# Keys of 30 heads in one load each, with the last 112 tiles copied aside by ScalarE

## The chip, the cores and the metric

The kernel runs on one core of a Trainium2 chip. The metric is the device time of one execution in microseconds (us). The median of three runs before the change is 1277.63 us (1277.61 to 1277.86).

## The reference

One token goes through a layer with attention over cached keys and values and then a small dense block. There are 32 heads of 128 elements and 32768 cached positions; the keys and the values of one head are 8 MB each in bf16, 537 MB in all.

```python
x = A_x                                              # 1 x 1 x 512
q = (layernorm(x) @ wq).reshape(32 heads, 128)
scores = einsum("bhqd,bhkd->bhqk", q, k_cache) * 128 ** -0.5
o = einsum("bhqk,bhkd->bhqd", softmax(scores), v_cache)
h = x + o.reshape(1, 1, 4096) @ wo                   # wo: 4096 x 512
t = layernorm(h) @ w1 + b1                           # w1: 512 x 1376
out = h + (t * tanh(softplus(t))) @ w2               # w2: 1376 x 512
```

## The kernel before

All large operands live in `ring`, six slots of 32 KB per partition. Slots 0 and 1 take the two halves of a head's keys, slots 2 and 3 its values, slot 4 first `wq` and at the end `w1` and `w2`, and slot 5 `wo`. Partition p holds 256 consecutive positions of the cache (`"(p r) d -> p (r d)"`), so a head's keys are 256 tiles of 128 x 128, 128 tiles in each half. A half is one load with 32 KB in a row per partition; the values of a head are one load with 64 KB in a row.

All large loads are issued by SyncE, in the order of the list `order`: `wq`, then for every head both halves of the keys and the values, then `wo` in four pieces, `w1` in two and `w2` in four. SyncE's queue (SPq in the profile) is strictly in order, so a load that waits holds back all behind it. `freed_by` says what a load waits for: a half of the keys for the last transposes of the same half of the head before, the values for the last matmul on the values of the head before (`pv`), `w1` and `w2` for the last use of `wq` (`qm32`). `wo` waits for nothing, since its slot is empty until then.

For each head (`one`, a loop over 32 heads in the programs of TensorE, VectorE and ScalarE) TensorE goes through 32 groups of eight tiles (`k_group`). It transposes the eight tiles (L456) into one of four PSUM buffers, VectorE copies them to `ering` (L459), and three groups later TensorE multiplies them with the query (L433, `scores`). Then come the maximum (L482 to L499), the exponential on ScalarE (L502), the sum (L507) and 256 matmuls of values with probabilities (L470, `pv`). In this loop ScalarE has nothing but the exponential. After the last head TensorE brings the 32 outputs into place (L535, L539) and runs `wo` (L549), the second layernorm, `w1` (L564) and `w2` (L583). POOL writes to a scratch row `skip` only in order to count a semaphore up where a load has one part instead of two.

Of the kernel before, what the change touches and what calls it, by code (L numbers as in the profile page):

```python
# [7 lines left out]
F32 = mybir.dt.float32  # L8
# [5 lines left out]
PE, ACT, DVE, POOL, SP = "pe", "act", "dve", "pool", "sp"  # L14
# [156 lines left out]
def build_kernel(nc, A_x, A_k_cache, A_v_cache, A_wq, A_wo, B_w1, B_b1, B_w2, out):  # L171
    D = A_x.shape[-1]
    Dh = 128
    HD = A_wq.shape[1]
    H = HD // Dh
# [9 lines left out]
    TPS = 128  # L185
    SLOT = TPS * Dh
    HALVES = Sk // (128 * TPS)
    SCOLS = HALVES * TPS
    GT = 8
    GPS = TPS // GT  # L190
    NE = 4
    NT = 4
    KEEP = 3
    FJ = F // 128
    FLAST = F - FJ * 128
    W1 = KC * F
# [7 lines left out]
    def sb(shape, dt, name):  # L204
        cm = nc.sbuf_tensor(name, shape, dt)
        t = cm.__enter__()
        allocs.append(cm)
        return t.ap()
# [7 lines left out]
    ring = sb([128, NS, SLOT], BF16, "ring")  # L216
# [4 lines left out]
    nb = sb([128, 1], F32, "nbias")  # L221
    esum = sb([128, 1], F32, "esum")
    pmax = sb([128, 1], F32, "pmax")
    rtotc = sb([128, 1], F32, "rtotc")
    gmax = sb([1, 1], F32, "gmax")
    skip = sb([1, H], F32, "skip")
    identi = sb([128, 128], I32, "identi")
    ident = sb([128, 128], F32, "ident")
    identb = sb([128, 128], BF16, "identb")
# [34 lines left out]
    OX_PS = T_f[2][:, 0:32]  # L264

    sem = nc.alloc_semaphore
    kinds = [PE, ACT, DVE, POOL, SP, "exp", "pmax", "gmax", "qc", "A", "B", "C", "pv", "nb", "rcp", "qm"]
    kinds += [f"{k}{i}" for i in range(2 * GPS) for k in ("ev", "tr", "qk")]
    sems = {k: sem(f"s_{k}") for k in kinds}
    ready = [sem(f"ready{i}") for i in range(NS)]  # L270
# [11 lines left out]

    order = [("wq", 0)]
    for h in range(H):
        order += [("k", h, half) for half in range(HALVES)]
        order.append(("v", h))
    order += [("wo", n) for n in range(len(s_wo))] + [("w1", n) for n in range(len(s_w1))] + [("w2", n) for n in range(len(s_w2))]

# [5 lines left out]
    def ready_wait(what):  # L294
        return (ready[slot_of(what)], 16 * (what[1] + 1 if what[0] in "kv" else 1))

    def free_name(what):
        return "free" + "_".join(map(str, what))

    def freed_by(what):  # L300
        if what[0] in ("w1", "w2"):
            return [f"qm{H}"]
        if what[0] in "kv" and what[1] > 0:
            return [free_name((what[0], what[1] - 1) + what[2:])]
        return []

    def flat_of(what):
        if what[0] == "v":
            return ring[:, HALVES:2 * HALVES, :].rearrange("p s x -> p (s x)")
        return ring[:, slot_of(what), :]  # L310

    def tiles_of(what):
        return flat_of(what).rearrange("p (r d) -> p r d", d=Dh)

    wq_v = ring[:, slot_of(("wq",)), :].rearrange("p (k n) -> p k n", k=KC)
    wo_f = ring[:, slot_of(("wo",)), :]
# [7 lines left out]
    def program(S):  # L324
        t_ = nc.tensor
        a = nc.scalar
        v = nc.vector
        g = nc.gpsimd
# [3 lines left out]
        def start(dst, src, s):  # L332
            S.dma(SP, lambda: sp.dma_start(dst, src).then_inc(s, 16))  # L333

        for what in order:
            slot = slot_of(what)
            S.wait(SP, freed_by(what))
            flat = flat_of(what)
            if what[0] == "wq":
                start(flat, A_wq.rearrange("(p k) n -> p (k n)", k=KC), ready[slot])  # L340
            elif what[0] == "wo":
                j0, j1 = WO_J[what[1]:what[1] + 2]
                start(wo_f[:, j0 * D:j1 * D], A_wo.rearrange("(p j) n -> p (j n)", j=32)[:, j0 * D:j1 * D], s_wo[what[1]])
            elif what[0] == "w1":
                k0, k1 = W1_K[what[1]:what[1] + 2]
                start(w1_v[:, k0:k1, :], B_w1[k0 * 128:k1 * 128, :].rearrange("(k p) n -> p k n", p=128), s_w1[what[1]])
            elif what[0] == "w2":
                j0, j1 = W2_J[what[1]:what[1] + 2]
                if j1 <= FJ:
                    start(w2_v[:, j0:j1, :], B_w2[j0 * 128:j1 * 128, :].rearrange("(j p) n -> p j n", p=128), s_w2[what[1]])  # L350
                else:
                    start(w2_v[0:FLAST, FJ, :], B_w2[FJ * 128:F, :], s_w2[what[1]])
            else:
                cache = A_k_cache if what[0] == "k" else A_v_cache
                rows = cache[0, what[1], :, :].rearrange("(p r) d -> p (r d)", r=SCOLS)
                at = what[2] * SLOT if what[0] == "k" else 0
                if what == ("v", H - 1):
                    start(flat[:, 0:SLOT], rows[:, 0:SLOT], ready[slot])
                    start(flat[:, SLOT:], rows[:, SLOT:], s_half)
                else:  # L360
                    start(flat, rows[:, at:at + flat.shape[-1]], ready[slot])
        S.dma(SP, lambda: sp.dma_start(out[0, 0, :].rearrange("(c m) -> c m", c=KC), outr[0:128:32, :]).then_inc(s_out, 16),
              waits=["fin"])
# [8 lines left out]
        if S.emit and S.only == POOL:  # L372
            for n in range(H - 1):
                g.memset(skip[:, n:n + 1], 0.0).then_inc(s_half, 16)
        S.step(POOL, lambda: g.iota(seli[:, :, :], [[-1, WB], [1, 128]], base=0, channel_multiplier=-WB), name="seli")
        S.step(POOL, lambda: g.memset(b1r[:, :], 0.0), name="b1z")
        S.dma(POOL, lambda: g.dma_start(b1r[0:FJ, :], B_b1[0:FJ * 128].rearrange("(j p) -> j p", j=FJ)).then_inc(s_b1, 16),
              waits=["b1z"])
        S.dma(POOL, lambda: g.dma_start(b1r[FJ:FJ + 1, 0:FLAST], B_b1[FJ * 128:F].rearrange("(o p) -> o p", o=1)).then_inc(s_b1, 16))
        S.step(DVE, lambda: v.memset(oT[:, :], 0.0), name="oTz")  # L380
        S.step(DVE, lambda: v.memset(onesm[:, :], 1.0), name="consts0")
        S.step(DVE, lambda: v.memset(epsc[:, :], EPS), name="epsc")
# [4 lines left out]
               waits=["identb", (s_x, 32)])  # L387
# [24 lines left out]
        for kc in range(KC):  # L412
            S.step(PE, lambda kc=kc: t_.matmul(Q_REG, wq_v[:, kc, 0:Dh], xnT[:, 0, kc:kc + 1], start=(kc == 0), stop=(kc == KC - 1)),
                   name=[f"qkb{kc - NE}"] + (["qm0"] if kc == KC - 1 else []), kind=f"qk{(kc - NE) % (2 * GPS)}",
                   waits=(["xn0", ready_wait(("wq", 0))] if kc == 0 else ()))
# [25 lines left out]
        def k_group(h, half, gi):  # L441
            what = ("k", h, half)
            bg = count[0]
            count[0] += 1
            kt = tiles_of(what)
            tb = T_b[bg % NT]
            for r in range(GT):
                waits = []
                if r == 0:
                    if gi == 0:  # L450
                        waits.append(ready_wait(what))
                    waits.append("identb")
                names = []
                if r == GT - 1:
                    names = [f"trb{bg}"] + ([free_name(what)] if gi == GPS - 1 else [])
                S.step(PE, lambda r=r: t_.matmul(tb[:, r * 128:(r + 1) * 128], kt[:, gi * GT + r, :], identb[:, :],  # L456
                                                 is_transpose=True, start=True, stop=True),
                       name=(names or None), waits=waits, kind=(f"tr{bg % (2 * GPS)}" if names else None))
            S.step(DVE, lambda: v.tensor_copy(ering[:, bg % NE, :, :].rearrange("p r d -> p (r d)"), tb[:, :]),  # L459
                   name=f"ev{bg}", waits=[f"trb{bg}", f"qkb{bg - NE}"],  # L460
                   kind=f"ev{bg % (2 * GPS)}")
            pend.append((h, half * TPS + gi * GT, bg))
            flush(KEEP)

# [46 lines left out]

        def one(n):
            h = n - 1
            for half in range(HALVES):
                for gi in range(GPS):
                    k_group(h, half, gi)
            flush(0)
            soft_max(h)
            soft_a(h)
            soft_b(h)  # L520
            soft_exp(h)
            pv(h, 0, 64)
            soft_c(h)
            pv(h, 64, SCOLS)
            oev(h)
# [5 lines left out]
        if S.emit and S.only == PE:  # L531
            S.hint = t_.mark_branch_hint_location("LikelyTaken")
        S.step(PE, lambda: t_.matmul(hid_ps, b1r[:, :], identb[0:FJ + 1, 0:FJ + 1], start=True, stop=False, skip_group_check=True),
               waits=[(s_b1, 32), f"exp{H - 1}"])
        S.step(PE, lambda: t_.matmul(OR_PS, oT[:, :], identb[:, :], is_transpose=True, start=True, stop=True),  # L535
               name="oRt", waits=[f"oev{H - 1}", "oTz"])
        S.step(DVE, lambda: v.tensor_copy(oR[:, :], OR_PS), name="oR", waits=["oRt"])
        for b in range(WB):
            S.step(PE, lambda b=b: t_.matmul(OX_PS, sel[:, b, :], oR[:, 32 * b:32 * b + 32], start=(b == 0), stop=(b == WB - 1)),  # L539
                   name=("oXs" if b == WB - 1 else None), waits=(["oR", "sel"] if b == 0 else ()))  # L540
        S.step(DVE, lambda: v.tensor_copy(oX[:, :], OX_PS), name="oX", waits=["oXs"])
        S.step(DVE, lambda: v.memset(hpad[:, :], 0.0), name="hpadz")
        for j in range(32):
            for c in range(KC):
                waits = ["oX"] if j == 0 and c == 0 else []
                if c == 0 and j in WO_J:
# [4 lines left out]
                    start=(j == 0 and c == 0), stop=last, skip_group_check=True),  # L551
                    name=("y" if last else None), waits=waits)
# [6 lines left out]
               waits=["hpad", f"exp{H - 1}"])  # L559
        for kc in range(KC):  # L560
            for j in range(FJ + 1):
# [4 lines left out]
                    start=False, stop=last, skip_group_check=True),  # L566
                    name=("hid" if last else None), waits=((["xn1"] if kc == 0 else []) + ([(s_w1[W1_K.index(kc)], 16)] if kc in W1_K else []) if j == 0 else ()))
# [8 lines left out]
        for j in range(FJ + 1):  # L576
# [4 lines left out]
            for c in range(KC):  # L581
# [51 lines left out]
```

## Time and profile before

| what | value |
|---|---|
| median of 3 runs | 1277.63 us |
| span of the profiled execution (its own time is given as this span alone) | 1275.6 us |
| bytes moved, mean rate over the span | 548.24 MB, 430 GB/s |
| TensorE busy with matmuls | 1020.0 us (80%) |
| VectorE busy | 716.0 us (56%) |
| ScalarE busy | 20.6 us (2%) |
| mean granted TensorE clock | 0.769 |

A row of the timeline has the start, the duration, the engine, the line, what is written and read and how many instructions are merged; in brackets stands the idle time before it and what ended that. "issue" is time in which an engine waited for nothing that the profile shows. A row of the chain of waits has the start, the duration and the work. In a row of groups the number behind the bar is the total busy time, then the mean of one instruction in ns. A row on a DMA queue has packets, MB and the time that the packets took, as a share of 16 engines over the stretch asked for; it exceeds 100% a little where packets overlap or reach over the stretch's end. A row of stretches gives the busy time of TensorE's matmuls, its weight loads, VectorE, ScalarE and POOL, then the granted clock, the DMA share and GB/s.

### The profile page before, as it was taken

To read this page: it belongs to the slowest core of one execution; us is meant where nothing else is said; L and a number is where in the kernel's file an instruction comes from. 1 tells how busy PE (TensorE), PEld (TensorE's weight loads), DVE (VectorE), ACT (ScalarE), POOL (GpSimd) and SP (SyncE) were. 2 spreads that over 40 slices of the span, in tenths; PEclk is the share of its full clock that TensorE was granted. 3 is DMA by queue.
4 is the path that set the end of the run, shared out by engine and by line. 5 is a ranking of instruction groups with operands and counts; after the bars stand their busy time and mean duration, and the time that the engine had idled before them with its cause. 6 is when DMAs were issued, how large, how long until landed. Compare 5 with 4: busy or idle time off the path is not lost.

```text
span 1275.6 us, 53362 instructions
## 1 busy us (share of the span) xinstructions
PE 1020.0 (80%) x25129; PEld 996.3 (78%) x25129; DVE 716.0 (56%) x1246; ACT 20.6 (2%) x70; POOL 3.3 (0%) x40
## 2 busy tenths in 40 slices
PE   3788877879777888777887778797778887788977
PEld 3688877879777878777887778797778887777876
DVE  3466544566545665445665446664456654456643
ACT  0000000000000000000000000000000000000000
POOL 1000000000000000000000000000000000000000
PEclk9788777787767887768886778877678877688866
DMA  9999999999999999999999999999999999999998
GB/s 417 416 429 439 434 434 428 432 432 439 432 436 424 436 432 439 432 428 428 438 442 430 427 430 431 437 444 427 430 428 432 440 439 427 424 434 433 438 427 350
DMA packets 16906, 548.24 MB, mean 430 GB/s; under 512 B 1952, under 2 KB 3328, under 8 KB 4096
## 3 DMA queue, kind: packets, MB, share of 16 engines
q1 hardware_dynamic: 16680, 548.09, 99.7%
q8 instruction: 8, 0.13, 0.0%
q10 hardware_dynamic: 152, 0.00, 0.0%
q0 software_dynamic: 64, 0.00, 0.0%
q14 instruction: 2, 0.02, 0.0%
HBM read 548.08 MB, written 0.00 MB: 430 GB/s over the span
## 4 chain that ended last, share of the span: by engine, by line
DMA 66%; PE 32%; SPq 1%; issue 1%; DVE 0%; ACT 0%; ACTq 0%
DMA ring<-in_A_k_cache_dram 65%; PE tps L456 25%; PE sps L433 6%; SPq L333 1%; DMA ring<-in_B_w_dram 1%; PE ops L470 1%; DVE ering L459 0%; PE hlp L492 0%; PE hlp L497 0%; PE tps L583 0%; DVE pmax L482 0%; PE hlp L507 0%; PE yps L485 0%; DVE ering L589 0%; DVE gmax L494 0%
## 5 line engine op out<-in xcount | busy, mean ns | idle before, releaser
L459 DVE COPY ering<-tps 128x1024 bf16<-128x1024 bf16 x1024 | 669.3, 691 | 129.3 <-PE tps L456 128.5
L456 PE MATMUL tps<-identb,ring 128*128 128x128 bf16 x8192 | 667.7, 232 | 76.4 <-DMA ring<-in_A_k_cache_dram 76.4
L456 PEld LDWEIGHTS tps<-identb,ring 128*128 128x128 bf16 x8192 | 522.0, 104 | 78.9 <-DMA ring<-in_A_k_cache_dram 78.9
L433 PE MATMUL sps<-qcur,ering 128*128 128x1 bf16 x8192 | 343.7, 164 | 11.0 <-DVE ering L459 6.7
L470 PEld LDWEIGHTS ops<-pbuf,ring 128*128 128x128 bf16 x8192 | 229.7, 105 | 134.4 <-issue 132.5
L470 PE MATMUL ops<-pbuf,ring 128*128 128x1 bf16 x8192 | 227.6, 165 | 132.4 <-DMA ring<-in_A_v_cache_dram 127.2
L433 PEld LDWEIGHTS sps<-qcur,ering 128*128 128x128 bf16 x8192 | 308.9, 97 | 14.0 <-DVE ering L459 9.4
L509 DVE RECIPROCAL rtotc<-hlp 128x1 f32<-128x1 f32 x32 | 5.4, 168 | 196.6 <-PE hlp L507 196.6
L477 DVE TENSOR_TENSOR oT<-ops,rtotc 128x1 f32 x32 | 5.1, 161 | 165.7 <-PE ops L470 165.7
L502 ACT ACTIVATE pbuf<-sps,nbias 128x256 bf16<-128x256 f32 x32 | 15.1, 473 | 1223.1 <-DVE nbias L499 1223.1
L497 PEld LDWEIGHTS hlp<-gmax,onesmat 1*128 1x128 f32 x64 | 12.0, 233 | 21.6 <-DVE gmax L494 21.6
L497 PE MATMUL hlp<-gmax,onesmat 1*128 1x1 f32 x64 | 14.8, 297 | 11.9 <-DVE gmax L494 11.9
L482 DVE TENSOR_REDUCE pmax<-sps 128x1 f32<-128x256 f32 x32 | 13.6, 424 | 14.3 <-PE sps L433 14.3
L507 PE MATMUL hlp<-esum,onesmat 128*128 128x1 f32 x64 | 18.1, 352 | 0.0
L485 PE MATMUL yps<-xnT,ring 128*128 128x1 bf16 x128 | 16.3, 172 | 0.0
L492 PE MATMUL hlp<-ident,pmax 128*1 128x128 f32 x64 | 12.4, 275 | 4.7 <-DVE pmax L482 3.4
L507 PEld LDWEIGHTS hlp<-esum,onesmat 128*128 128x128 f32 x64 | 16.1, 312 | 0.0
L494 DVE TENSOR_REDUCE gmax<-hlp 1x1 f32<-1x128 f32 x32 | 8.9, 279 | 11.9 <-PE hlp L492 11.9
L499 DVE TENSOR_SCALAR nbias<-hlp 128x1 f32<-128x1 f32 x32 | 5.0, 158 | 17.7 <-PE hlp L497 17.7
L485 PEld LDWEIGHTS yps<-xnT,ring 128*128 x128 | 12.3, 96 | 2.0
L492 PEld LDWEIGHTS hlp<-ident,pmax 128*1 128x1 f32 x64 | 2.7, 80 | 7.4 <-DVE pmax L482 7.4
L386 PE MATMUL hlp<-identb,xr 4*128 4x4 bf16 x1 | 0.2, 159 | 9.3 <-DMA xr<-in_A_x_dram 9.3
(61 smaller groups left out, 41.2 us busy)
## 6 DMA issues: line engine op xcount, KB each, us to landing
ring<-in_A_k_cache_dram SPq DMA_DIRECT2D x64, 4096.0 KB, 26.7
ring<-in_A_v_cache_dram SPq DMA_DIRECT2D x2, 4096.0 KB, 26.2
ring<-in_A_wq_dram SPq DMA_DIRECT2D x1, 4096.0 KB, 12.3
ring<-in_A_wo_dram SPq DMA_DIRECT2D x1, 1792.0 KB, 34.7
ring<-in_B_w_dram SPq DMA_DIRECT2D x2, 688.0 KB, 17.5
ring<-in_A_wo_dram SPq DMA_DIRECT2D x1, 1280.0 KB, 37.4
ring<-in_B_w_dram SPq DMA_DIRECT2D x2, 512.0 KB, 19.6
ring<-in_A_wo_dram SPq DMA_DIRECT2D x1, 768.0 KB, 38.8
```

Source lines behind the costliest of these rows:

```text
L333: S.dma(SP, lambda: sp.dma_start(dst, src).then_inc(s, 16))
L433: S.step(PE, lambda r=r: t_.matmul(S_ps[:, col0 + r:col0 + r + 1], ering[:, bg % NE, r, :], qcur[:, :], start=True, stop=True), name=(name ...
L456: S.step(PE, lambda r=r: t_.matmul(tb[:, r * 128:(r + 1) * 128], kt[:, gi * GT + r, :], identb[:, :], is_transpose=True, start=True, stop= ...
L459: S.step(DVE, lambda: v.tensor_copy(ering[:, bg % NE, :, :].rearrange("p r d -> p (r d)"), tb[:, :]), name=f"ev{bg}", waits=[f"trb{bg}", f ...
L470: S.step(PE, lambda r=r, last=last: t_.matmul(o_ps[:, 0:1], vt[:, r, :], pbuf[:, r:r + 1], start=(r == 0), stop=last), name=([free_name((" ...
L482: S.step(DVE, lambda: v.tensor_reduce(pmax[:, :], S_ps[:, 0:SCOLS], AXX, ALU.max), name=f"pmax{h}", waits=[f"qkh{h}"], kind="pmax")
L485: S.step(PE, lambda kc=kc: t_.matmul(Q_REG, wq_v[:, kc, bass.ds((S.index(h + 1) % H) * Dh, Dh)], xnT[:, 0, kc:kc + 1], start=(kc == 0), st ...
L492: S.step(PE, lambda: t_.matmul(A_REG, pmax[:, :], ident[:, :], start=True, stop=True), name=f"A{h}", waits=[f"pmax{h}", "ident"], kind="A")
L494: S.step(DVE, lambda: v.tensor_reduce(gmax[:, :], A_REG, AXX, ALU.max), name=f"gmax{h}", waits=[f"A{h}"], kind="gmax")
L497: S.step(PE, lambda: t_.matmul(B_REG, onesm[0:1, :], gmax[:, :], start=True, stop=True), name=f"B{h}", waits=[f"gmax{h}", "consts0"], kind ...
L502: S.step(ACT, lambda: a.activation(pbuf[:, :], S_ps[:, 0:SCOLS], ACTF.Exp, bias=nb[:, :], scale=SC, accum_out=esum[:, :]), name=f"exp{h}", ...
L507: S.step(PE, lambda: t_.matmul(C_REG, onesm[:, :], esum[:, :], start=True, stop=True), name=f"C{h}", waits=[f"exp{h}"], kind="C")
```

## The change

The keys of heads 1 to 30 come in one load over slots 0 and 1, with 64 KB in a row per partition. The first and the last head (0 and 31) keep two halves. For every head, also for these two, ScalarE copies the last 112 of the 256 tiles to slot 5, as soon as all keys of the head are there and TensorE is through with the copy of the head before. TensorE transposes groups 0 to 17 from the slots of the load and groups 18 to 31 from the copy. The next load of keys waits for the transposes of group 17 (`kfree`) and for the copy (`kc`). The loads of `wo`, whose slot is now in use, wait for the last transposes of the last head (`kend31`). POOL counts the second half's semaphore up for the 30 heads that have no second load.

```diff
+    CT = 112
+    CG = (2 * TPS - CT) // GT
...
-        order += [("k", h, half) for half in range(HALVES)]
+        order += [("k", h, half) for half in range(HALVES if h in (0, H - 1) else 1)]
...
-        if what[0] in "kv" and what[1] > 0:
-            return [free_name((what[0], what[1] - 1) + what[2:])]
+        if what[0] == "wo":
+            return [f"kend{H - 1}"]
+        if what[0] == "k" and what[1] > 0:
+            return [f"kfree{what[1] - 1}", f"kc{what[1] - 1}"]
+        if what[0] == "v" and what[1] > 0:
+            return [free_name((what[0], what[1] - 1))]
...
+    khome = ring[:, 0:HALVES, :].rearrange("p s x -> p (s x)")
+    kcopy = ring[:, 2 * HALVES + 1, 0:CT * Dh]
...
+                if what[0] == "k" and 0 < what[1] < H - 1:
+                    start(khome, rows, ready[slot])
...
+        S.wait(POOL, [(ready[1], 16)])
+        if S.emit and S.only == POOL:
+            for n in range(1, H - 1):
+                g.memset(skip[:, H + n:H + n + 1], 0.0).then_inc(ready[1], 16)
...
-            kt = tiles_of(what)
+            g0 = half * GPS + gi
+            kt = kc_tiles if g0 >= CG else k_tiles
+            t0 = (g0 - (CG if g0 >= CG else 0)) * GT
...
+                    if g0 == CG:
+                        waits.append(f"kc{h}")
...
+            S.step(ACT, lambda: a.copy(kcopy, khome[:, CG * GT * Dh:]), name=f"kc{h}", kind="kc",
+                   waits=[(ready[0], 16 * (h + 1)), (ready[1], 16 * (h + 1))] + [f"kend{h - 1}"])
```

On ScalarE, in the loop over heads, the program before has the exponential alone:

```order
L407 ACTIVATE lns<-lns 128x1 [waits s_act]
L93 UNCONDITIONAL_BRANCH
L502 ACTIVATE pbuf,esum<-sps,nbias 128x256 [waits s_nb]
L93 REGISTER_ALU
L93 COMPARE_AND_BRANCH
```

The changed program has the copy ahead of it (`s_tr31` counts the last transposes of a head, `ready0` and `ready1` the two halves' loads):

```order
L425 ACTIVATE lns<-lns 128x1 [waits s_act]
L93 UNCONDITIONAL_BRANCH
L93 ISA
L536 COPY ring<-ring 128x14336 [waits s_tr31,ready1,ready0]
L524 ACTIVATE pbuf,esum<-sps,nbias 128x256 [waits s_nb]
L93 REGISTER_ALU
L93 COMPARE_AND_BRANCH
```

The copy stands ahead of the exponential of the same head and waits for loads and for TensorE, not for VectorE.

On SyncE's queue the last loads before the change are these (`s_tr15` counts the last transposes of a first half, `s_pv` the end of a head's values, `s_qm` the last use of `wq`):

```order
L333 DMA ring<-in_A_k_cache_dram 128x16384 [waits s_tr15]
L333 DMA ring<-in_A_k_cache_dram 128x16384 [waits s_tr31]
L333 DMA ring<-in_A_v_cache_dram 128x16384 [waits s_pv]
L333 DMA ring<-in_A_v_cache_dram 128x16384
L333 DMA ring<-in_A_wo_dram 128x7168
L333 DMA ring<-in_A_wo_dram 128x5120
L333 DMA ring<-in_A_wo_dram 128x3072
L333 DMA ring<-in_A_wo_dram 128x1024
L333 DMA ring<-in_B_w_dram 128x2x1376 [waits s_qm]
```

In the changed program the same stretch, with the last whole load of keys and its values ahead, reads:

```order
L344 DMA ring<-in_A_k_cache_dram 128x32768 [waits s_kc,s_tr17]
L344 DMA ring<-in_A_v_cache_dram 128x32768 [waits s_pv]
L344 DMA ring<-in_A_k_cache_dram 128x16384 [waits s_kc,s_tr17]
L344 DMA ring<-in_A_k_cache_dram 128x16384
L344 DMA ring<-in_A_v_cache_dram 128x16384 [waits s_pv]
L344 DMA ring<-in_A_v_cache_dram 128x16384
L344 DMA ring<-in_A_wo_dram 128x7168 [waits s_tr31]
L344 DMA ring<-in_A_wo_dram 128x5120
L344 DMA ring<-in_A_wo_dram 128x3072
L344 DMA ring<-in_A_wo_dram 128x1024
L344 DMA ring<-in_B_w_dram 128x2x1376 [waits s_qm]
```

The two halves of the last head's keys are issued together, behind the copy of the head before, and the first piece of `wo` has a wait where it had none.

More of the change, by code (lines that the diff above doesn't have):

```diff
@@ L225, in build_kernel @@
     gmax = sb([1, 1], F32, "gmax")
-    skip = sb([1, H], F32, "skip")
+    skip = sb([1, 2 * H], F32, "skip")
     identi = sb([128, 128], I32, "identi")
@@ L266, in build_kernel @@
     sem = nc.alloc_semaphore
-    kinds = [PE, ACT, DVE, POOL, SP, "exp", "pmax", "gmax", "qc", "A", "B", "C", "pv", "nb", "rcp", "qm"]
+    kinds = [PE, ACT, DVE, POOL, SP, "exp", "pmax", "gmax", "qc", "A", "B", "C", "kc", "pv", "nb", "rcp", "qm"]
     kinds += [f"{k}{i}" for i in range(2 * GPS) for k in ("ev", "tr", "qk")]
@@ L313, in tiles_of @@
         return flat_of(what).rearrange("p (r d) -> p r d", d=Dh)
+    khome = ring[:, 0:HALVES, :].rearrange("p s x -> p (s x)")
+    kcopy = ring[:, 2 * HALVES + 1, 0:CT * Dh]
+    k_tiles = khome.rearrange("p (r d) -> p r d", d=Dh)
+    kc_tiles = kcopy.rearrange("p (r d) -> p r d", d=Dh)
     wq_v = ring[:, slot_of(("wq",)), :].rearrange("p (k n) -> p k n", k=KC)
@@ L356, in program @@
                 at = what[2] * SLOT if what[0] == "k" else 0
-                if what == ("v", H - 1):
+                if what[0] == "k" and 0 < what[1] < H - 1:
+                    start(khome, rows, ready[slot])
+                elif what == ("v", H - 1):
                     start(flat[:, 0:SLOT], rows[:, 0:SLOT], ready[slot])
@@ L374, in program @@
                 g.memset(skip[:, n:n + 1], 0.0).then_inc(s_half, 16)
+        S.step(POOL, lambda: g.memset(skip[:, H - 1:H], 0.0), name="kend-1", kind=f"tr{2 * GPS - 1}")
         S.step(POOL, lambda: g.iota(seli[:, :, :], [[-1, WB], [1, 128]], base=0, channel_multiplier=-WB), name="seli")
@@ L454, in k_group @@
                 if r == GT - 1:
-                    names = [f"trb{bg}"] + ([free_name(what)] if gi == GPS - 1 else [])
-                S.step(PE, lambda r=r: t_.matmul(tb[:, r * 128:(r + 1) * 128], kt[:, gi * GT + r, :], identb[:, :],
+                    names = [f"trb{bg}"] + ([f"kfree{h}"] if g0 == CG - 1 else []) + ([f"kend{h}"] if g0 == 2 * GPS - 1 else [])
+                S.step(PE, lambda r=r: t_.matmul(tb[:, r * 128:(r + 1) * 128], kt[:, t0 + r, :], identb[:, :],
                                                  is_transpose=True, start=True, stop=True),
```

## The prediction

> **What bounds the kernel now.** I read the page first, then the chain and the waits, then one middle head, the first head and the last one in the timeline.
>
> ```profile
> span 1275.6 us, 53362 instructions
> DMA  9999999999999999999999999999999999999998
> DMA packets 16906, 548.24 MB, mean 430 GB/s; under 512 B 1952, under 2 KB 3328, under 8 KB 4096
> DMA 66%; PE 32%; SPq 1%; issue 1%; DVE 0%; ACT 0%; ACTq 0%
> ...
> PE ops L470 <- DMA ring<-in_A_v_cache_dram: 127.2, 30, 4.8
> ...
> PE tps L456 <- DMA ring<-in_A_k_cache_dram: 76.4, 31, 9.4
> ```
>
> The transfers run in every slice and TensorE waits about twice per head, once for keys and once for values, some 4.2 and 2.5 us. Two rows of the chain, 29 heads apart, give the beat, each being the first matmuls on a head's first half of keys:
>
> ```profile
> 101.90 3.60 PE tps L456 x32
> ...
> 1226.48 3.59 PE tps L456 x32
> ```
>
> (1226.48 - 101.90) / 29 = 38.78 us per head for 16.8 MB, so a half of the keys takes about 9.7 and the values 19.4 us. What TensorE does with a head fits into that with some room. The timeline of a middle head shows how much:
>
> ```profile
> 606.01 3.60 PE L456 MATMUL tps<-identb,ring 128*128 128x128 bf16 x32 [2.23 <-DMA ring<-in_A_k_cache_dram]
> ...
> 610.71 18.16 DVE L459 COPY ering<-tps 128x1024 bf16<-128x1024 bf16 x28 [0.38 <-PE tps L456]
> ...
> 612.01 0.61 PE L456 MATMUL tps<-identb,ring 128*128 128x128 bf16 x8
> ...
> 617.82 10.67 SPq L333 DMA_DIRECT2D ring<-in_A_k_cache_dram  x2
> ...
> 628.92 0.35 PE L433 MATMUL sps<-qcur,ering 128*128 128x1 bf16 x8 [0.21 <-DVE ering L459]
> ...
> 631.15 0.47 ACT L502 ACTIVATE pbuf<-sps,nbias 128x256 bf16<-128x256 f32 x1 [37.77 <-DVE nbias L499]
> ...
> 635.16 1.84 PE L470 MATMUL ops<-pbuf,ring 128*128 128x1 bf16 x64 [4.24 <-DMA ring<-in_A_v_cache_dram]
> ...
> 637.30 5.26 PE L470 MATMUL ops<-pbuf,ring 128*128 128x1 bf16 x192
> ...
> 642.59 0.33 SPq L333 DMA_DIRECT2D ring<-in_A_v_cache_dram  x1
> ...
> 644.78 3.56 PE L456 MATMUL tps<-identb,ring 128*128 128x128 bf16 x32 [2.23 <-DMA ring<-in_A_k_cache_dram]
> ...
> 1251.93 0.47 ACT L502 ACTIVATE pbuf<-sps,nbias 128x256 bf16<-128x256 f32 x1 [38.88 <-DVE nbias L499]
> ...
> 1252.55 1.87 PE L470 MATMUL ops<-pbuf,ring 128*128 128x1 bf16 x64 [0.85 <-ACT pbuf L502]
> ...
> 606.00:616.00 10.00, 9.99 (x186) 10.00 (x187) 8.06 (x13) 0.00 (x0) 0.00 (x0) 0.77 1.12 485
> ```
>
> From the keys' arrival (606.01) the scores are done after 23.26 us (629.27). A group of eight tiles goes by every 18.16 / 28 = 0.649 us; the group at 612.01 is the eighth, so the start costs 6.00 us for seven groups where 4.54 would do, 1.46 us more. The last row, of the table by stretches, has the reason: over the first ten microseconds the granted clock was 0.77 of full. I call this the slow start and count it again after every stop of some microseconds. The eighteenth group's transposes are over at 612.01 + 10 x 0.649 + 0.61 = 619.1, or 13.1 us after arrival. The stage on the values takes 637.30 + 5.26 - 635.16 = 7.40 us; in the last head (the last two rows), where the values were there in time, it began 0.62 us behind the exponential's start.
>
> **The change part by part.** *The loads.* I compare the queue in a stretch that holds halves of keys only (packets of 32 KB) and one with values only (64 KB), each of known length:
>
> ```profile
> q1 hardware_dynamic: 80, 2.62, 101.5%
> ...
> q1 hardware_dynamic: 80, 5.24, 100.9%
> ```
>
> The first answer is for 606.5 to 612.5 us, the second for 617 to 629. A packet took 1.015 x 16 x 6 / 80 = 1.218 us and 1.009 x 16 x 12 / 80 = 2.4216 us. Two small ones are dearer than one large by 14 ns, rounding leaving 1 ns either way per row. An engine's share of a head is 16 small and 8 large packets, 38.86 us by these times against a beat of 38.78, so packets overlap by 3.4 ns at each of 24 joints. With 16 large packets the beat is 16 x (2.4216 - 0.0034) = 38.69 us: 0.09 us less, and 30 such heads give back 2.6 us (1.5 to 3.5 by the rounding). That is all the change can gain while the queue stays full.
>
> *Does it stay full in a middle head?* The keys now arrive at once, 9.7 us later against the beat than their first half did, and TensorE starts that much later. It no longer waits for values, which land 19.4 us after the keys while the scores take 23.3. So TensorE ends a head 631.15 + 0.62 - 606.01 + 7.40 = 33.2 us after the keys' arrival. The next values are issued there, and the queue needs them at 38.7: 5.5 us of cover. Now it is 11.9 us (issued at 642.59, due when the second half lands at 644.78 + 9.7). The next keys wait for group 18 (13.1) and the copy, and are needed at 19.4. So no idle queue, if the copy is near 13 us or shorter.
>
> *The copy.* One ScalarE instruction over 14336 elements per partition; no such operation is in the trace. The nearest rows:
>
> ```profile
> L502 ACT ACTIVATE pbuf<-sps,nbias 128x256 bf16<-128x256 f32 x32 | 15.1, 473 | 1223.1 <-DVE nbias L499 1223.1
> ...
> L405 ACT ACTIVATE lns<-lns,epsc 128x1 f32<-128x1 f32 x2 | 0.6, 294 | 22.8 <-DVE lns L403 22.8
> L407 ACT ACTIVATE lns<-lns 128x1 f32<-128x1 f32 x2 | 0.4, 202 | 0.1
> ```
>
> 256 elements cost 473 ns. Against the one-element row with a bias operand the slope is (473 - 294) / 255 = 0.70 ns, against the one of the same function 1.06 ns. That is 10.3 or 15.4 us for the copy, with the 0.2 us of the short row. Neither row is nearer (one shares the operands, the other the function), so I take the middle, 12.8, and keep both ends. In a middle head it then ends before group 18 and costs nothing; at 15.4 TensorE would stand 2.4 us there. The Trainium skill's page "ScalarE: Activation LUTs", section "What ACT_TABLE_LOAD costs", gives 186 ns plus 0.833 ns per element whatever the function; by it the copy is an estimated 12.1 us and the sum below would be 0.7 us less. No run so far shows such a copy.
>
> *The first head* still has halves, so the copy starts only with the second, and TensorE has eighteen groups behind it long before the copy ends.
>
> ```profile
> 36.51 0.61 PE L456 MATMUL tps<-identb,ring 128*128 128x128 bf16 x8
> ...
> 50.29 0.35 PE L433 MATMUL sps<-qcur,ering 128*128 128x1 bf16 x8 [0.21 <-DVE ering L459]
> ...
> 59.64 3.48 issue
> ...
> 64.75 0.33 SPq L333 DMA_DIRECT2D ring<-in_A_v_cache_dram  x1
> ...
> ring<-in_A_wq_dram SPq DMA_DIRECT2D x1, 4096.0 KB, 12.3
> ```
>
> The nineteenth group ran at 36.51. The third head's first half landed at 101.90; one load of values and one of keys earlier, 29.1 us, the second head's second half landed (72.8), and one beat before that the first head's (34.0). The copy ends near 47. Fourteen groups from there, 9.1 us plus 1.46 for a slow start, and 1.1 to the last scores: 58.7 against 50.6. From scores to the end of the values' stage 14.1 us passed, so the second head's values would be issued at 72.8, just where its keys land. The queue would idle for the start of a transfer, at most the 12.3 - 9.7 = 2.6 us by which a load on an empty queue is longer. But 3.48 us of those 14.1 were a stop for "issue", and the long wait may cover that. So 0 to 2.6; I take 1.0. The Trainium skill's "Runtime: NRT & Kernel Launch", section "Instruction fetch mechanics", has the next block of instructions fetched while the current one runs, with the crossing mostly hidden; the row of 3.48 us disagrees for the first round, and by the rule with the wait in front the cost would be 0 and the sum 1.0 us less.
>
> *The last head* also comes in halves, and here nothing hides the copy.
>
> ```profile
> 1225.12 1.85 SPq L333 DMA_DIRECT2D ring<-in_A_wo_dram  x4
> ...
> 1249.70 0.35 PE L433 MATMUL sps<-qcur,ering 128*128 128x1 bf16 x8 [0.21 <-DVE ering L459]
> ...
> 1261.48 2.74 PE L549 MATMUL yps<-oX,ring 128*128 128x1 bf16 x96 [0.28 <-DVE oX L541]
> 1264.89 1.05 PE L549 MATMUL yps<-oX,ring 128*128 128x1 bf16 x32 [0.67 <-DMA ring<-in_A_wo_dram]
> ```
>
> Let X be the landing of its first half, now 1226.48. Scores end at 1250.05, X + 23.6. After the change the head before has its keys at X - 29.1 and TensorE leaves it at X + 4.1. Seventeen to eighteen groups: X + 17.2. The second half lands at X + 9.7, so the copy ends at X + 22.6, a signal's 0.1 us included: a stop of 5.4 us. Then 9.1 + 1.46 us: the last transposes at X + 33.2, the last scores at X + 34.3, 10.7 later than now. The wo loads, now issued 1.4 us ahead of X, wait for those last transposes, and behind them on SP's queue stand the six loads of w1 and w2. The values landed at X + 29.1, so the queue runs dry for 4 us and more; a 4 MB load then takes 12.3 us, so wo is there at X + 45.5. TensorE reaches it 11.4 us after its scores, at X + 45.7, a tie, and the present wait of 0.67 us goes. The tail is 10.0 us longer. w1 and w2 follow the queue and are not last.
>
> Sum: -2.6 + 1.0 + 10.0 = +8.4 us on 1275.6, so a span of 1284.0. The page gives no time of its own beside the span; the runs' median, 1277.63, is 2.0 us above it, which I take as lying around it: 1286.0. With the copy at 10.3 us the tail is 2.5 shorter, 1.5 more if that stop is too short to slow TensorE's start, and the first head is free: 1281.0 to 1282.5. At 15.4 us it is 2.6 longer and the first head costs 3.6: 1291.2.
>
> **The rivals.** *Values too late.* With a slow copy every middle head stops at group 19. The head then ends 33.2 + 2.4 + up to 1.5 = 37.1 us after its keys, and a load that needs up to 2.6 us to start misses 38.7 by 1.0. The idle queue delays the next keys too, which gives that head the time back, so half is lost per head: 0.5 x 30 = 15 us, 1306. It decides where stop and slow start pass 2.9 us, that is with a copy over 15 us. For it: the slope of 1.06. Against: it needs every end at once.
>
> *The copy hides everywhere.* At 7.4 us or less (0.5 ns per element) the last head doesn't stop; its scores end at X + 4.1 + 23.26, 3.8 later than now, less 0.67 for wo: 1277.63 - 2.6 + 3.1 = 1278.1, within what a measurement can tell from no change (0.2%, 2.6 us). No row supports that slope.
>
> *Faster, by the loads.* If a load of a head's keys gained much more than its packets show, all the rest could be paid. It decides at (10.0 + 1.0 + 2.6) / 30 = 0.45 us a load; at 0.6 us the time is 1277.63 + 11.0 - 18 = 1270.6. Against it stand the values, which move in such packets today: 0.45 us is 56 ns for each of 8, where the rows show 11.
>
> *No larger packets.* If the new loads were cut at 32 KB, the 2.6 us don't come: 1288.6. The values' row (5.24 MB in 80 packets) speaks against it.
>
> **How the numbers follow.** The forecast with its ends, 1281 to 1291, has 0.73, the uncut gain missing included; values too late 0.12; hidden copy 0.10; faster by the loads 0.05. The first two are slower by more than 0.2%, and so is a small part of the third (1280.2 is the bound): slower 0.87, same 0.08, faster 0.05. The range from 1279.5 to 1294 takes in the forecast, the upper part of the hidden copy and the mild end of the late values.
>
> **What would show it.** Right: 64 KB packets on all middle keys, a beat of 38.69 us, a copy of 10 to 15 us, no wait of TensorE for values in middle heads, a longer one for keys (about 5.5 us); in the last head a stop of TensorE for ScalarE of about 5 us, wo issued some 33 us after the first half, and a dip of DMA near the end. Wrong: a beat over 38.8 (then values are late), a copy under 8 us, or no dip before wo.

## The result and the profile after

The changed kernel takes 1287.82 us (median of 4 runs, 1286.7 to 1289.63) against 1277.62 us before (1277.56 to 1277.86): a ratio of 1.0081 with a 95% interval of 1.0066 to 1.0096. It is slower by 10.2 us; 1286.0 was forecast. The profiled execution took 1288.06 us, its span is 1285.2.

The page of the changed kernel, and below it two rows of its waits (who waited for what: total us, times, longest):

```profile
span 1285.2 us, 53459 instructions
DMA  9999999999999999999999999999999999999996
DMA packets 12586, 548.23 MB, mean 427 GB/s; under 512 B 1472, under 2 KB 2848, under 8 KB 3616
L536 ACT COPY ring<-ring 128x14336 bf16<-128x14336 bf16 x32 | 388.4, 12139 | 431.0 <-DMA ring<-in_A_k_cache_dram 417.7
...
PE tps L478 <- DMA ring<-in_A_k_cache_dram: 176.4, 31, 9.3
...
PE tps L478 <- ACT ring L536: 14.2, 2, 9.7
```

The packets fell from 16906 to 12586. The wait for values is gone from TensorE's list and the one for keys grew from 76.4 to 176.4 us, some 5.6 in each middle head. The copy takes 12.14 us in every head, but only twice in 32 heads did TensorE wait for it: 9.7 us in the first head and 4.5 in the last. The DMA row is full but for its last slice. The chain of waits gives the beat, and shows one head that is out of step:

```profile
152.11 3.60 PE tps L478 x32
191.20 3.60 PE tps L478 x32
...
268.57 3.60 PE tps L478 x32
...
1197.91 3.59 PE tps L478 x32
```

From 268.57 to 1197.91 there are 24 heads, 38.72 us each, against 38.78 before; from 152.11 to 191.20 it was 39.09. A middle head in the timeline:

```profile
616.86 12.14 ACT L536 COPY ring<-ring 128x14336 bf16<-128x14336 bf16 x1 [13.51 <-DMA ring<-in_A_k_cache_dram]
616.88 3.59 PE L478 MATMUL tps<-identb,ring 128*128 128x128 bf16 x32 [6.06 <-DMA ring<-in_A_k_cache_dram]
...
630.13 0.33 SPq L344 DMA_DIRECT2D ring<-in_A_k_cache_dram  x1
...
642.79 1.86 PE L492 MATMUL ops<-pbuf,ring 128*128 128x1 bf16 x64 [0.85 <-ACT pbuf L524]
...
650.24 0.33 SPq L344 DMA_DIRECT2D ring<-in_A_v_cache_dram  x1
...
655.59 3.59 PE L478 MATMUL tps<-identb,ring 128*128 128x128 bf16 x32 [5.38 <-DMA ring<-in_A_k_cache_dram]
```

The copy starts with TensorE and ends (629.00) before group 18 is over (630.13, when the next keys are ordered). The values' stage follows the exponential at once. The next values are ordered 33.4 us after the keys' landing and 5.3 us ahead of the next landing of keys. The first head:

```profile
46.42 1.03 PE L478 MATMUL tps<-identb,ring 128*128 128x128 bf16 x8 [9.68 <-ACT ring L536]
...
58.39 0.35 PE L451 MATMUL sps<-qcur,ering 128*128 128x1 bf16 x8 [0.21 <-DVE ering L481]
...
70.40 1.61 PE L492 MATMUL ops<-pbuf,ring 128*128 128x1 bf16 x55 [3.29 <-issue]
...
72.04 0.33 SPq L344 DMA_DIRECT2D ring<-in_A_v_cache_dram  x1
...
72.80 3.37 PE L478 MATMUL tps<-identb,ring 128*128 128x128 bf16 x32 [0.79 <-DMA ring<-in_A_k_cache_dram]
```

TensorE stood 9.7 us for the copy, scores ended at 58.74 instead of 50.64, the stop for "issue" (3.29 us) is still there, and the second head's values were ordered only 0.8 us ahead of the landing of its keys. The last head, and the DMA row of the last 46 us in 40 slices:

```profile
1230.83 3.59 PE L478 MATMUL tps<-identb,ring 128*128 128x128 bf16 x32
...
1236.72 12.14 ACT L536 COPY ring<-ring 128x14336 bf16<-128x14336 bf16 x1 [13.23 <-issue]
...
1248.91 1.03 PE L478 MATMUL tps<-identb,ring 128*128 128x128 bf16 x8 [4.47 <-ACT ring L536]
...
1259.73 1.83 SPq L344 DMA_DIRECT2D ring<-in_A_wo_dram  x4
...
1260.49 0.35 PE L451 MATMUL sps<-qcur,ering 128*128 128x1 bf16 x8 [0.21 <-DVE ering L481]
...
1272.26 3.57 PE L573 MATMUL yps<-oX,ring 128*128 128x1 bf16 x128 [0.28 <-DVE oX L565]
...
DMA  9999999999992000019999999999999997000000
```

The second half of the keys lands at 1236.7, so X, the landing of the first half, is 1227.0. TensorE comes to the head at X + 3.8, stops 4.5 us for the copy, and ends its scores at X + 33.8. wo is ordered at X + 32.7, and the queue is dry for some 5 us before it.

### The profile page after: what moved, and what is told of

It reads as the page before. It is cut to its first block, busy times and chain, and to the rows that moved or that the text cites. A ratio compares the mean times of both kernels' runs of the same rounds, so it can differ in the third digit from the quotient of the medians.

```text
span 1285.2 us, 53459 instructions
## 1 busy us (share of the span) xinstructions
PE 1022.0 (80%) x25129; PEld 998.0 (78%) x25129; DVE 716.0 (56%) x1246; ACT 409.0 (32%) x102; POOL 4.4 (0%) x71
## 4 chain that ended last, share of the span: by engine, by line
DMA 64%; PE 32%; ACT 2%; issue 1%; DVE 0%; SPq 0%; ACTq 0%; DVEq 0%
DMA ring<-in_A_k_cache_dram 64%; PE tps L478 25%; PE sps L451 6%; ACT ring L536 2%; PE ops L492 1%; PE yps L573 0%; PE sps L588 0%; PE tps L607 0%; SPq L344 0%; DVE ering L481 0%; PE hlp L414 0%; DVE pmax L504 0%; PE hlp L529 0%; PE hlp L514 0%; PE hlp L519 0%
## 5 line engine op out<-in xcount | busy, mean ns | idle before, releaser
L478 PE MATMUL tps<-identb,ring 128*128 128x128 bf16 x8192 | 669.8, 232 | 190.6 <-DMA ring<-in_A_k_cache_dram 176.4
L536 ACT COPY ring<-ring 128x14336 bf16<-128x14336 bf16 x32 | 388.4, 12139 | 431.0 <-DMA ring<-in_A_k_cache_dram 417.7
L492 PEld LDWEIGHTS ops<-pbuf,ring 128*128 128x128 bf16 x8192 | 229.4, 105 | 33.2 <-ACT pbuf L524 29.9
L492 PE MATMUL ops<-pbuf,ring 128*128 128x1 bf16 x8192 | 228.0, 165 | 30.5 <-ACT pbuf L524 27.2
L507 PEld LDWEIGHTS yps<-xnT,ring 128*128 x128 | 12.2, 95 | 2.2
## 6 DMA issues: line engine op xcount, KB each, us to landing
ring<-in_A_k_cache_dram SPq DMA_DIRECT2D x4, 4096.0 KB, 23.4
ring<-in_B_w_dram SPq DMA_DIRECT2D x2, 512.0 KB, 15.7
```

What stands on the lines that cost most here:

```text
L492: S.step(PE, lambda r=r, last=last: t_.matmul(o_ps[:, 0:1], vt[:, r, :], pbuf[:, r:r + 1], start=(r == 0), stop=last), name=([free_name((" ...
L507: S.step(PE, lambda kc=kc: t_.matmul(Q_REG, wq_v[:, kc, bass.ds((S.index(h + 1) % H) * Dh, Dh)], xnT[:, 0, kc:kc + 1], start=(kc == 0), st ...
L536: S.step(ACT, lambda: a.copy(kcopy, khome[:, CG * GT * Dh:]), name=f"kc{h}", kind="kc", waits=[(ready[0], 16 * (h + 1)), (ready[1], 16 * ( ...
```

## Experiments

The theory: middle heads cost nothing, the loss lies in the copies of the first and the last head and in the late start of the last. The rival: the copy disturbs loads or TensorE in every head.

**The ends one by one.** The last 112 tiles of chosen heads are loaded straight to slot 5 by a third load, and ScalarE only signals their landing. `DIRECT` lists these heads, `PARTS` the heads whose keys come in halves. Not shown below: ScalarE's loop over the heads is split where such a head stands.

```diff
+                elif what[0] == "k" and what[1] in DIRECT and what[2] == 1:
+                    cut = CG * GT * Dh
+                    start(khome[:, SLOT:cut], rows[:, SLOT:cut], ready[slot])
+                    S.wait(SP, [f"kend{what[1] - 1}"])
+                    start(kcopy, rows[:, cut:], s_kb)
...
+            if h in DIRECT:
+                S.step(ACT, lambda: a.copy(tiny[:, :], epsc[:, :]), name=f"kc{h}", kind="kc",
+                       waits=[(s_kb, 16 * (DIRECT.index(h) + 1)), "epsc"])
```

Head 0 alone (`DIRECT = (0,)`):

> The last 112 tiles of head 0's keys are loaded straight to slot 5, and ScalarE only signals; all else is as in the changed kernel. Theory of the two ends (the loss lies in the first and the last head alone): TensorE does not stop at group 19 of head 0, its scores end near 50.6 us instead of 58.7, the second head's values are issued near 65 instead of 72.0, ahead of the landing of its keys, and the last head's first half lands 2 to 3 us earlier than 1227.0. Time 1285 to 1286. Rival (the copy disturbs loads or TensorE in every head): no change beyond 0.5 us.

Measured: 1284.16 us (1283.94 to 1284.83), 3.7 less than the changed kernel. Timeline and chain:

```profile
63.03 1.60 PE L521 MATMUL ops<-pbuf,ring 128*128 128x1 bf16 x55 [3.48 <-issue]
...
64.66 0.33 SPq L368 DMA_DIRECT2D ring<-in_A_v_cache_dram  x1
...
72.66 3.60 PE tps L507 x32
111.35 3.59 PE tps L507 x32
```

The values are ordered 8 us ahead of the keys' landing, and the beat is 38.69 from the second head on. By the landing records (the trace has one for each of the 16 DMA engines of a load; the last of them is the load's landing) the last head's first half lands at 1224.0, 2.9 us ahead of the changed kernel, as expected. The gain in time is larger than the theory expected by about 1 us.

Head 31 alone:

> The same for head 31 alone: its last 112 tiles are loaded straight to slot 5. Theory of the two ends: the stop of 4.5 us and the slow start behind it go, the last scores come about 27.4 us after the last head's first half instead of 33.8, wo is issued before the values have landed, so the queue does not run dry. Time 6 to 7 us less than the changed kernel: 1281 to 1282. Rival (copy disturbs every head): under 1 us less.

Measured: 1280.75 us (1279.41 to 1283.5), 7.1 less, a little more than the theory had.

Both:

> Heads 0 and 31 both. Theory of the two ends: the two gains add, 1278 to 1279.5; what remains against the kernel before is the late start of the last head (3.8 us less 0.7) less the loads' gain (1.7 to 2.6). Rival (copy disturbs every head): 1286 to 1288.

Measured: 1278.06 us (1277.18 to 1278.82); the ratio to the kernel before is 1.0004 (0.9994 to 1.0013). The two gains add up (10.7 apart, 9.8 together), and the rival falls: the 30 middle heads still copy. The last head now reads:

```profile
1228.45 3.17 PE L507 MATMUL tps<-identb,ring 128*128 128x128 bf16 x32
...
1249.76 1.76 SPq L368 DMA_DIRECT2D ring<-in_A_wo_dram  x4
```

TensorE comes to it at 1228.45 without a wait, late because the keys of head 30 came whole; wo is ordered 10 us earlier than in the changed kernel.

**The late start.** Head 30 is loaded directly too (`DIRECT = PARTS = (0, H - 2, H - 1)`):

> As the kernel with heads 0 and 31 loaded directly, and head 30 in the same way (halves, last 112 tiles straight to slot 5). Theory: what is left in the tail there is the late start, 4.2 us after the last head's first half, because the keys of head 30 come whole. With halves TensorE is through with head 30 by then and the tail is that of the kernel before (49.1 us from the landing). Landing of the last head's first half near 1224.5 (2 us before that of the kernel before), so a span near 1273.6 and a time of 1275.6 to 1276.4, 0.1 to 0.15% faster than before. Rival (the tail is set by something else, for instance the wait of the first piece of wo): as with two heads, 1278.

Measured: 1275.63 us (1275.43 to 1276.13, 11 runs), ratio 0.9985 (0.9976 to 0.9994), span 1273.7. The chain:

```profile
111.61 3.60 PE tps L507 x32
...
1156.54 3.57 PE tps L507 x32
...
1224.46 3.59 PE tps L507 x32
```

TensorE starts the last head with the landing at 1224.46, 2.0 us ahead of the kernel before, and the rest takes 49.2 us as there (49.1). This version is 2.0 us faster than the kernel before and 12.2 us faster than the changed one; the 2.0 us are what the loads gain. The beat is (1156.54 - 111.61) / 27 = 38.70.

**The packets.** The change as it is, but with keys in two loads of 32 KB rows for all heads:

```diff
-        order += [("k", h, half) for half in range(HALVES if h in (0, H - 1) else 1)]
+        order += [("k", h, half) for half in range(HALVES)]
```

> As the changed kernel, copy included, but the keys of all heads come as two loads with 32 KB in a row, issued together. Theory (64 KB packets are worth 0.06 to 0.09 us per head): the beat goes from 38.72 back to 38.78 or 38.8, and the time is 1.7 to 2.6 us longer, 1289.5 to 1290.5. Rival (the packet size is worth nothing, the beat of the changed kernel has another reason): beat 38.72, time as the changed kernel.

Measured: 1288.70 us (1288.56 to 1292.66), less than expected, and its runs overlap with those of the changed kernel, so the times alone decide little. The edit also does more than it was meant to: the first half is there 9.7 us ahead of the second again, TensorE starts with it, and so it stops for the copy in 31 heads (137.0 us in all). The traces decide. The copies start with the landing of each head's second half; first and last start stand in the views of the copies, of the changed kernel and of this one:

```profile
L536 ACT COPY ring<-ring x32: 12138/12139/12142, 34.2 to 1236.7; 128x14336 bf16<-128x14336 bf16 x32
```

```profile
L530 ACT COPY ring<-ring x32: 12138/12139/12141, 34.0 to 1238.7; 128x14336 bf16<-128x14336 bf16 x32
```

1204.7 against 1202.5 us for the same bytes: the 64 KB rows are worth 2.2 us, 0.07 per head. Both stretches hold the late order behind the first head. Free of it are the middle heads: by the landing records of heads 4 to 28 a head's keys land 19.43 us after the values ahead of them here and in the kernel before, and 19.35 in the changed kernel (medians), 0.08 less. The rival, that packets are worth nothing, falls.

**How much cover the middle heads have.** ScalarE copies some columns once more ahead of each copy; nothing of the result changes.

```diff
+            S.step(ACT, lambda: a.copy(kcopy[:, 0:4096], khome[:, CG * GT * Dh:CG * GT * Dh + 4096]), name=f"kx{h}", kind="kx",
+                   waits=[(ready[0], 16 * (h + 1)), (ready[1], 16 * (h + 1))] + [f"kend{h - 1}"])
```

> As the changed kernel, but ScalarE first copies 4096 of the 14336 columns once more, about 3.6 us on top (a wait added, nothing of the result changed). Theory of the cover: in middle heads the copy ends 15.8 us after the keys' landing, TensorE stops 2.7 us at group 19, ends the head 36 to 37.4 us after the landing, still ahead of 38.7, so the beat stays at 38.7 to 38.75. The two ends get the 3.6 us in full: 7 us in all, 1294 to 1296. Rival (values too late, no cover left): a beat over 39 and a time above 1300.

Measured: 1336.61 us (1334.1 to 1338.69). The theory missed by 41 us. A head in the timeline shows where:

```profile
601.02 3.60 PE L478 MATMUL tps<-identb,ring 128*128 128x128 bf16 x32 [2.95 <-DMA ring<-in_A_k_cache_dram]
...
616.83 1.03 PE L478 MATMUL tps<-identb,ring 128*128 128x128 bf16 x8 [2.56 <-ACT ring L538]
...
628.98 0.35 PE L451 MATMUL sps<-qcur,ering 128*128 128x1 bf16 x8 [0.21 <-DVE ering L481]
...
639.19 0.33 SPq L344 DMA_DIRECT2D ring<-in_A_v_cache_dram  x1
...
640.42 3.25 PE L478 MATMUL tps<-identb,ring 128*128 128x128 bf16 x32 [1.26 <-DMA ring<-in_A_k_cache_dram]
```

The stop is 2.6 us as expected, but the fourteen groups behind it take 12.5 us to the last score, 2.3 more than without a stop (10.2): five of these groups take 1.07 us instead of 0.65, while the granted clock is 0.50. So the values are ordered 38.2 us after the landing. This order stands 1.2 us ahead of the landing at 640.4. By the landing records of this trace most orders of values in heads 4 to 28 stand 2 to 4 us ahead (19 of 25; all lie between 1.2 and 4.9), and the values land 20.6 us after the keys on average and up to 21.8, where 19.35 is the transfer: orders that the theory took for early enough cost up to 2.5 us.

Twice that:

> The same with 8192 columns copied once more, about 7.0 us on top. Theory of the cover: the stop is 6.1 us in every middle head and the start behind it slow, 40.8 us from the landing of the keys to the issue of values, 2.1 past the beat, and a transfer needs about 1.3 us to start; the delay of one head gives the next one time, so the beat grows by about half of 3.4, to 40.4, and the time to about 1350 (1287.8 + 14 at the two ends + 29 x 1.7). Rival (only the ends count): 1302.

Measured: 1378.19 us (2 runs), 28 more than the theory. Together the two say that an order must come much earlier than the 1.3 us I had allowed, an estimate that no run shows. The changed kernel itself shows one late order in full: the values ordered at 72.04 landed, by the landing records, at 93.91, 21.9 us later, where a transfer in a full queue takes 19.35: 2.5 us on top. In the records of the changed kernel and of the two runs with extra columns the first of the 16 engines reports a load 0.4 to 3.1 us before the last, and an engine that is through has nothing to do until the next order. With some 2 us for this that makes 4 to 4.5 us, tried next on the version with three direct heads, whose ends are clean. Extra columns 2048 and 3072:

> The kernel with three heads loaded directly (1275.6), where only middle heads copy, with 2048 columns copied once more ahead of each copy, 1.9 us. TensorE stops about 1 us at group 19 and the next values are issued some 4.6 us ahead of the landing of the keys instead of 5.5. Theory (the queue needs an order 4 to 4.5 us ahead: 2.6 from issue to landing beyond the transfer, and about 2 by which the first of the 16 engines is through before the last): no loss, beat 38.70 to 38.75, 1275.5 to 1277.5. Rival (any wait of TensorE in a middle head is paid in full): 1 us a head, about 1305.

Measured: 1276.74 us (1276.15 to 1277.6), 1.1 more than without.

```profile
532.83 0.33 SPq L368 DMA_DIRECT2D ring<-in_A_v_cache_dram  x1
...
537.33 3.59 PE L507 MATMUL tps<-identb,ring 128*128 128x128 bf16 x32 [4.53 <-DMA ring<-in_A_k_cache_dram]
...
576.04 3.59 PE L507 MATMUL tps<-identb,ring 128*128 128x128 bf16 x32 [4.34 <-DMA ring<-in_A_k_cache_dram]
```

An order 4.5 us ahead loses nothing here: the beat is 38.71. In the landing records of this execution, the slowest of ten, three loads lose 1.6 us together; they were ordered 4.2 to 5.2 us ahead.

> The same with 3072 columns, 2.75 us: the stop is about 1.8 us, and if TensorE's start behind it is slow, the values are issued 2.5 to 3.7 us ahead. Theory of 4 to 4.5 us: part of the heads lose 0.5 to 1 us, beat 39.0 to 39.7, 1285 to 1305. Rival (1.3 to 2.6 us ahead is enough): 1275.6 to 1277.

Measured: 1301.71 us (1294.06 to 1304.86).

```profile
508.55 3.60 PE L507 MATMUL tps<-identb,ring 128*128 128x128 bf16 x32 [4.37 <-DMA ring<-in_A_k_cache_dram]
...
543.60 0.33 SPq L368 DMA_DIRECT2D ring<-in_A_v_cache_dram  x1
...
547.66 3.60 PE L507 MATMUL tps<-identb,ring 128*128 128x128 bf16 x32 [4.09 <-DMA ring<-in_A_k_cache_dram]
```

Here the order is 4.1 us ahead of a landing that is itself late, 39.1 us after the one before; in 29 heads 26 us are lost, 0.9 each. TensorE's stop for the copy is 0.94 us on average with 2048 columns (27.2 us in 29 heads) and 1.89 with 3072 (54.8), so less than a microsecond separates the two.

**The same from the keys' side.** 88 tiles instead of 112 on the changed kernel (`CT = 88`):

> One number of the change is altered: 88 tiles are copied instead of 112 (CT), so TensorE reads 21 groups from the load and 11 from the copy. Theory of the two ends: the copy takes 14336/11264 less, about 9.5 us; in the last head it ends 19.2 us after the first half's landing, when TensorE is just through with group 20 (4.2 us of late start and 15.1 us), so the stop of 4.5 us and its slow start go; in head 0 the scores end 3 to 5 us earlier and the second head's values are issued ahead of the landing of its keys. The middle beat stays at 38.70, since group 20 is over 15.1 us after the keys land and the next keys are needed at 19.4. Time 1278 to 1279.5, as with the tiles of both end heads loaded directly. Rival (the shorter cover for the next keys' load shows): beat over 38.75 and a time above 1280.

Measured: 1281.62 us (1280.69 to 1285.89), ratio 1.0043 (1.003 to 1.0057). Its row of waits for the copy:

```profile
PE tps L478 <- ACT ring L536: 5.3, 1, 5.3
```

The stop in the last head is gone, as expected, and 6 us with it; the one left is head 0's. But the time is 2 to 4 us above the theory and the runs lie 5 us apart. With the keys ordered three groups later, by the landing records 3.7 to 5.1 us ahead of the values' landing, it is at the edge found above: the third head's, 3.7 us ahead behind the first head's delay, lost 0.9 us, one at 3.8 lost 0.4 and one at 3.7 nothing; what sets the spread of the runs was not tried further. Past the edge, on the version with three direct heads, `CT = 80`:

> The kernel with three heads loaded directly, with 80 tiles copied instead of 112, so 22 groups are read from the load and the next keys are issued only behind group 22, 15.8 us after the landing, 3.6 us ahead of the values' landing instead of 6.2. The values' order is as early as before. Theory of 4 to 4.5 us: the same loss from the other side, 0.3 to 1 us a head, beat 39.0 to 39.7, 1285 to 1305. Rival (only the order of the values matters): 1275.6.

Measured: 1291.16 us (1289.43 to 1299.05).

```profile
509.81 3.59 PE L507 MATMUL tps<-identb,ring 128*128 128x128 bf16 x32 [6.66 <-DMA ring<-in_A_k_cache_dram]
...
526.01 0.33 SPq L368 DMA_DIRECT2D ring<-in_A_k_cache_dram  x1
...
549.84 3.60 PE L507 MATMUL tps<-identb,ring 128*128 128x128 bf16 x32 [6.37 <-DMA ring<-in_A_k_cache_dram]
```

The keys are ordered 16.2 us after the landing, 3.2 ahead of the end of the values (19.35), and the next landing is 40.0 us after the last. The rival, that only the order of the values matters, falls. The losses of this trace's loads against 19.35 us (heads 1 to 30) add up to 23.2 us, and its execution (1299.05) is 23.4 longer than the 1275.63 without the edit; with 3072 columns it is 27.2 of 27.5.

Worked out from the landing records of seven traces (the changed kernel, `CT = 88`, 4096 columns, and the four last versions with three direct heads), heads 4 to 28, this is what an order's lead over the landing ahead of it means for its own transfer:

| order ahead of the landing, to the nearest 0.5 us | values: loads, mean loss us | keys: loads, mean loss us |
|---|---|---|
| 2.5 | 11, 1.75 | none |
| 3.5 | 5, 1.24 | 9, 0.90 |
| 4.0 | 21, 0.53 | 23, 0.30 |
| 4.5 | 23, 0.04 | 28, 0.10 |
| 5.5 | 49, 0.01 | 16, 0.11 |

Leads of other sizes are left out. The edge lies at about 4 us for both; it is not sharp, as single loads lost nothing at 4.0 and up to 0.8 us at 4.5.

The packet records show in part why 4. In the trace with `CT = 80` the keys ordered at 526.01 have their first packets at 526.97, 0.96 us later, when the first engine had been through with the values since 526.30, and the first six of these packets take 2.9 to 3.4 us instead of 2.42. So it matters when the first engine is through, and not only the last: over the loads of the table's traces (all leads), an order less than 2 us ahead of the first engine's landing record lost 1.07 us on average (64 loads), an earlier one 0.06 (286). No run varied the spread of the engines alone.

## Why the prediction was right, and where not

- **Loads, -2.6 forecast:** the comparison of traces with small packets gave 2.2, the beat of the version with three direct heads is 38.70 where 38.69 was forecast, and that version ends 2.0 below the kernel before. Right, the gain 0.4 too high.
- **Middle heads, 0 forecast:** right. The end of a head came 33.4 us after the landing (33.2 forecast), the cover was 5.3 (5.5), and with both end heads repaired the middle copies cost nothing.
- **The copy, 12.8 us forecast from 10.3 to 15.4:** 12.14, so the middle of the two slopes was near by luck: neither row was this operation. By the rate on the Trainium skill's page "ScalarE: Activation LUTs", section "What ACT_TABLE_LOAD costs", the copy is an estimated 12.13, and the trace agrees.
- **First head, +1.0 forecast from 0 to 2.6:** this term was mis-sized; taking it out gained 3.7 (2.9 between the landings of the last head's first half in the two traces). The order came at 72.04, near the 72.8 reckoned. The stop for "issue" that the wait was to cover stayed (3.29 us against 3.48). The wait did cover earlier ones: those of 1.70 and 1.98 us in the kernel before are gone. In the packet records a packet of 16 KB on an instruction queue starts in the stop that stayed (at 67.92; it began at 67.11), so TensorE probably waited for instructions there; no run tested it. The Trainium skill's page "Runtime: NRT & Kernel Launch", section "Instruction fetch mechanics", calls such crossings mostly hidden; this one was not, so the cost of 0 that was worked out by that rule did not come. And the price of a late order was counted as a delay of one landing: by the landing records the late values lost 1.8 us, and three of the loads soon behind them lost 0.5 more together (39.09 at 191.20). The kernels that keep this copy spread by 2.9 us (changed), 4.1 (head 31 direct) and 5.2 (`CT = 88`) over their runs, those without it (head 0 direct, both, three) by 0.9, 1.6 and 0.7; what sets the spread stays open.
- **Last head, +10.0 forecast:** the span behind X grew from 49.1 to 1285.2 - 1227.0 = 58.2, so 9.1. Its parts came as said: late start 3.8 (4.1), stop 4.5 (5.4, of a copy 0.7 longer), wo ordered at X + 32.7 (33.2) behind a dry queue, no wait of TensorE for wo. By the runs 7.1 us belonged to the copy and 2.4 to the late start.
- **Values too late:** the rival didn't come about, but its working was wrong. It was to begin at 2.9 us of stop and slow start and to cost 15 us with a copy of 15.4; copies of 15.7 together (with 4096 columns more) cost 49, an estimated 42 of it in the middle heads if the two ends take the 7 expected. The step that failed is the 2.6 us for a transfer's start: here the queue needed its order some 4 to 4.5 us ahead. The changed kernel stood about 1 us from that edge, and the upper end of the range was too low for that case.

Forecast and result thus agree within 1.8 us. The place and the kind of the loss were right, but that the sum is so near is in part luck: the first head was put 2.7 too low, the last 0.9 too high.

## What to carry to other kernels

While the queue stayed full, the change paid by its loads' price and nothing else, here 2 us; look first at the rounds where the steady state does not hold. What hides a new step in the middle of a loop can be missing in the first and the last round, and loads ordered behind those come late. And leave more between an order and its need than the latency of one load: here 4 to 4.5 us where the latency was 2.5.

## What the runs showed of the hardware

- A load ordered at 72.04, 0.7 us before the one ahead of it landed, took 2.5 us longer from order to landing than the 19.35 of its transfer in a full queue, and its first packets came 0.96 us after the order. But with 8 MB loads in turn a load lost 0.3 to 0.5 us on average when its order came 4 us ahead, and at most 0.1 at 4.5. The Trainium skill's page "DMA: Bandwidth & Descriptors", section "Anatomy of one DMA — SWDGE (gpsimd) path", has a fixed cost of about 2.0 us for loads that GpSimd issues; the loads here are SyncE's, and an order by that lead alone would be late.
- 0.9 us more of a wait can cost 25 us: 1276.74 with 2048 extra columns, 1301.71 with 3072.
- After a stop of 2.6 us fourteen groups took 2.3 us longer, more than the 1.46 that the start of a head costs. In both stretches the granted clock was 0.50 at first: for about 5.9 us behind the stop and about 4.6 us at the head's start. Why the one is longer is not shown.
